# Four of the 23 word conversions moved beside the second expert, the rest spread evenly

## The chip, the cores and the metric

The program runs on one core of one Trainium2 chip. The metric is device microseconds of one execution. Three executions of the kernel before gave 713.09, 840.9 and 712.39 us; the median is 713.09 us. All times inside the kernel come from one further, profiled execution.

## The reference, cut to what matters

Three stages follow one another. A gated linear attention makes x, 3072 tokens of 384 numbers. A mixture of eight experts sends each token to the one with the largest gate logit. A gated perceptron takes the result of that:

```python
# mixture of experts, for the tokens of expert e
h = np.maximum(x[mask] @ w1[e], 0.0)            # 384 -> 1024
out[mask] = gate_w[mask, None] * eom[mask, e, None] * (h @ w2[e])   # 1024 -> 384
# perceptron
a = x @ w1; b = x @ w2                          # 384 -> 1024 each
out = ((a * b) @ w3) @ w_out                    # 1024 -> 1024 -> 384
```

The perceptron's four weights reach the kernel as 64-bit floats. Each has to be rebuilt as a 32-bit float from its high and its low word before it can be used; this is the word conversion that the change moves.

## The kernel before, in words

**Arithmetic.** Every product after the attention is made with three matmuls of a high and a low part (`mm3`, L168 to L171). So each weight tile is split first: `feed` (L150) copies a 128x768 tile on ScalarE (L159) and subtracts on VectorE (L160). Activations are split in the same way (`x_split` L845 and L846, `h_split` L854 and L855).

**Order.** The order of every engine's instructions is the order in which the Python program emits them; nothing is reordered later. Each engine works through its own queue in that order, and the first instruction that waits holds all behind it. The SyncE queue (SP) issues the loads in the same way, and GpSimd (POOL) issues the gathers and the stores of converted words.

**The loop over experts (L1077).** Expert `e` has eight steps "up" (`e_up`, nine matmuls each, into one of three PSUM tiles `u`) and eight steps "down" (`e_down`, nine matmuls each). The number of columns falls from 464 to 360 with the expert (`CAPS`). In the down steps f = 1, 3 and 5 the tokens of the next expert are transposed on TensorE and split; the up steps of the next expert need all three. Expert 0 has its up steps elsewhere. After expert 6, `w_prime` (L1041) multiplies w3 and w_out into `wpr`, 64 blocks of three matmuls. Then comes expert 7, and then the perceptron (L1172), which is TensorE alone but for small work beside it.

**Side work.** Between steps, `next(conv)` emits the next piece of a generator. During experts 0 and 1 that is `late_routing` (gates, one-hot tiles `sohl` on VectorE at L715, and a sorting product on TensorE at L722, which is emitted in down step 5 of expert 1). From expert 2 on it is `convert_all`: 23 conversions in turn, each in four pieces:

- piece 1: ScalarE takes the absolute value of the high words (L132, "Abs");
- piece 2: VectorE clamps, shifts and joins them (L134, L135, L136, "the join");
- piece 3: nothing;
- piece 4: ScalarE scales the low words (L139), SP issues the load for the conversion after next (L958), GpSimd adds (L141) and issues the store of the tile to `wm_d` in DRAM (L962).

The raw words come into two buffers (`mr`), the results lie in two (`cva`), the scaled low words in one (`cvc`). The converted tiles are read back from `wm_d` by L120, from expert 5 on, as the weights of `w_prime` and of the perceptron. Before the change, a piece is emitted at each of the 16 steps of experts 2 to 4, at 12 of the 16 steps of experts 5 and 6, at every second block of the first three rows of `w_prime`, and at three blocks in eight of the next four. So experts 2, 3 and 4 hold four conversions each, experts 5 and 6 three, and the rest falls to `w_prime`.

**Rooms.** `wpr` has the pool `wprp` (L673) to itself, 12 KB of each partition, and is not written before `w_prime`. After expert 1 the routing's pools are closed (L1118) and the conversion's buffers take their place.

Of the kernel before, what the change touches and what calls it, by code (L numbers as in the profile page):

```python
# [7 lines left out]
F32 = mybir.dt.float32  # L8
F32R = mybir.dt.float32r
BF16 = mybir.dt.bfloat16  # L10
I32 = mybir.dt.int32
U32 = mybir.dt.uint32
ACTF = mybir.ActivationFunctionType
ALU = mybir.AluOpType
# [9 lines left out]
E = 8  # L24
F = 1024
KF = F // 128
# [5 lines left out]
TINY = 2.0 ** -15  # L32
NPC = 768
# [2 lines left out]
DP = 64  # L36
NP = 3
N_WO, N_W3, N_M, N_RING = 4, 11, 8, 8
N_D = N_WO + N_W3 + N_M

GMX = 6
# [15 lines left out]
def attention_then_moe_kernel(ctx, tc, pk0, pka, pkb, wbd_d, wexp, wmlp, cst_d, out):  # L57
    nc = tc.nc
    V, A, G, T, SP = nc.vector, nc.scalar, nc.gpsimd, nc.tensor, nc.sync
# [18 lines left out]
    jxB = const.tile([128, NJ], BF16, name="jxB")  # L78
    wm_d = dram.tile([N_D, 128, NPC], F32, name="wm_d")
    x_d = dram.tile([NTOK, DM], F32, name="x_d")  # L80
# [12 lines left out]
    def runits(a, b):  # L93
        return [("r", i, dkeys[i:min(i + 2, b)]) for i in range(a, b, 2)]

    def sunits(e):
        return [("s", 4 * e + u, [("e", e, 2 * u), ("e", e, 2 * u + 1)]) for u in range(4)]

    units = [u for e in range(E - 1) for u in sunits(e)] + runits(0, N_WO + N_W3)
    units += sunits(E - 1) + runits(N_WO + N_W3, N_D)  # L100
    Y_FIRST, Y_END = 6, len(units) - (N_M + 1) // 2
    assert Y_END % 4 == 0
    stream = [(u, c, key) for u, un in enumerate(units) for c, key in enumerate(un[2])]
    wmlp_w = wmlp.bitcast(I32)
# [3 lines left out]
    def load_ahead():  # L108
        while loaded[0] < min(freed[0] + (4 if Y_FIRST <= loaded[0] < Y_END + 2 else pools["keep"]), pools["upto"]):
# [14 lines left out]
            raws[loaded[0]] = raw  # L124
            loaded[0] += 1

    def words(raw, read):
        w = raw.rearrange("p (n t) -> p n t", t=2)
        lw, hw = w[:, :, 0], w[:, :, 1]
        a, c = [pools["cv"].tile([128, NPC], I32, tag=t, name="cv" + t, bufs=n) for t, n in (("a", 2), ("c", 1))]  # L130
        af = a.bitcast(F32)
        A.activation(out=af, in_=hw.bitcast(F32), func=ACTF.Abs)  # L132
        yield
        V.tensor_scalar(out=af, in0=af, scalar1=TINY, scalar2=None, op0=ALU.max)  # L134
        V.tensor_scalar(out=a, in0=a, scalar1=3, scalar2=0x3FFFFFF8, op0=ALU.logical_shift_left, op1=ALU.bitwise_and)  # L135
        V.scalar_tensor_tensor(out=a, in0=hw, scalar=-(1 << 30), in1=a, op0=ALU.bitwise_and, op1=ALU.bitwise_or)  # L136
        yield
        yield
        A.activation(out=c, in_=lw.bitcast(U32), func=ACTF.Copy, scale=2.0 ** -29)  # L139
        read()  # L140
        G.tensor_tensor(out=a, in0=a, in1=c, op=ALU.add)  # L141
        return a.bitcast(F32)
# [412 lines left out]
    for j in range(NJ):  # L555
# [30 lines left out]
        if j == 5:  # L586
            A.activation(out=row, in_=cst[:, C_E4:C_E4 + E], func=ACTF.Copy, scale=1024.0)
            V.scalar_tensor_tensor(out=revc, in0=cst[:, C_E4:C_E4 + E], scalar=-1024.0 * E, in1=rev, op0=ALU.mult,
                                   op1=ALU.add)
# [27 lines left out]
    def k_up(q, fs=range(2), low_last=False):  # L617
# [4 lines left out]
        for part in ((0, 1), (2,)) if low_last else ((0, 1, 2),):  # L622
            for f, k, sl in blocks:
                for i in part:
# [31 lines left out]
                    op=ALU.mult)  # L656
# [3 lines left out]
    for q in range(1, 4):  # L660
# [3 lines left out]
                    op=ALU.is_equal)  # L664
# [8 lines left out]
    wpr_p = ctx.enter_context(tc.tile_pool(name="wprp", bufs=1, reuse_waits="tile"))  # L673
# [9 lines left out]
    def rtile(shape, name, dt=F32):  # L683
        return rt_p.tile(shape, dt, name=name)
# [121 lines left out]
    def places(os_, big):  # L806
        V.tensor_scalar(out=zs, in0=zs, scalar1=1.0, scalar2=None, op0=ALU.add)
        yield
        V.tensor_tensor(out=pos, in0=pos, in1=key, op=ALU.add)
        V.reciprocal(out=zs, in_=zs)  # L810
        yield
        V.tensor_tensor(out=zs, in0=zs, in1=se, op=ALU.mult)
        yield
        sp = [rtile([128, NJ], f"sp{i}", BF16) for i in range(3)]
        V.tensor_copy(out=sp[0], in_=zs)
        yield
        V.tensor_tensor(out=zs, in0=zs, in1=sp[0], op=ALU.subtract)
        yield
        V.tensor_copy(out=sp[1], in_=zs)
        yield  # L820
        V.tensor_tensor(out=zs, in0=zs, in1=sp[1], op=ALU.subtract)
        yield
        V.tensor_copy(out=sp[2], in_=zs)
        yield
        yield from onehots(pos, iotaB[:, 0:NJ], sp, "s", os_, big)
# [55 lines left out]
    for f in range(KF):  # L881
        w = pieces["e", 0, f // 2]
# [21 lines left out]
    def late_routing(big):  # L904
        os_ = []
        yield from gates()
        yield from places(os_, big)
        yield
        yield
        ps_o = ps_u.tile([128, CMX], F32, tag="u", name="u")[:, 0:5 * NJ].rearrange("p (n h) -> p n h", n=5)  # L910
        sorted_mm(ps_o.rearrange("p n h -> p (n h)"), *os_)
        so = rtile([128, 5, NJ], "so")
        A.activation(out=so, in_=ps_o, func=ACTF.Copy)
        V.scalar_tensor_tensor(out=idx_o, in0=so[:, 0, :], scalar=128.0, in1=so[:, 1, :], op0=ALU.mult, op1=ALU.add)
        G.tensor_tensor(out=s2, in0=so[:, 2, :], in1=so[:, 3, :], op=ALU.add)
        G.tensor_tensor(out=s2, in0=s2, in1=so[:, 4, :], op=ALU.add)
        G.tensor_tensor(out=s2, in0=s2, in1=s2, op=ALU.mult)
# [34 lines left out]

    mraw = {}

    def m_load(i):
        if i < N_D:
            mraw[i] = pools["mr"].tile([128, 2 * NPC], I32, tag="mr", name="mraw")
            SP.dma_start(out=mraw[i], in_=wmlp_w[i])  # L958
# [82 lines left out]
    def w_prime():  # L1041
        wpr = wpr_p.tile([128, KF, DM], F32, tag="wpr", name="wpr")
        for f in range(KF):
            ps = ps_u.tile([128, CMX], F32, tag="u", name="u")[:, 0:DM]
            for g in range(KF):
                blk = f * KF + g
                hl, o = pieces["3", blk // 6], slice(blk % 6 * 128, blk % 6 * 128 + 128)
                so = slice(g % 2 * DM, (g % 2 + 1) * DM)
                wo = pieces["o", g // 2]
                mm3(ps, hl[:, 0, o], hl[:, 1, o], wo[:, 0, so], wo[:, 1, so], g == 0, g == KF - 1)  # L1050
                if blk % 6 == 5:
                    pieces.pop(("3", blk // 6))
                    if blk // 6 < N_W3 - 4:
                        feed(1)
                if f == KF - 1 and g % 2:
                    pieces.pop(("o", g // 2))
                    feed(1)
                if g % 2 if f < 3 else f < KF - 1 and g in (1, 4, 7):
                    next(conv, None)
            A.activation(out=wpr[:, f], in_=ps, func=ACTF.Copy)  # L1060
        pieces.pop(("3", N_W3 - 1))
        return wpr


    pl_p = lr.enter_context(tc.tile_pool(name="pl", bufs=1, reuse_waits="tile"))
    conv = late_routing(pl_p.tile)
    cv2 = ExitStack()

    def convert_all():
        m_load(0)  # L1070
        m_load(1)
        for _ in range(3):
            yield
        for i in range(N_D):
            yield from m_convert(i)

    for e in range(E):  # L1077
        if e == 1:
            interleave(windows())
        for f in range(KF if e else 0):  # L1080
            e_up(e, f, pieces["e", e, f // 2])
            if f % 2:
                pieces.pop(("e", e, f // 2))
            if (f % 2 if e < E - 1 else 3 <= f < 7):
                feed(1)
            if e < 5 or e < E - 1 and f % 2 == 0:
                next(conv, None)
        if e == E - 1:
            col = off_of(e)
            for d in range(KD):  # L1090
                feed((2, 2, 0)[d])
                for f in range(KF):
                    e_down(e, f, pieces["e", e, 4 + f // 2], [d])
                e_store(e, col, [d])
                y_split(0, [d])
            for f in range(4):
                pieces.pop(("e", e, 4 + f))
            break
        if e == 0:
            feed(1)  # L1100
        for f in range(KF):
            e_down(e, f, pieces["e", e, 4 + f // 2])
            if f % 2:
                pieces.pop(("e", e, 4 + f // 2))
                feed(1)
            if e == 0 and f in (0, 2) or 2 <= e < 6 and f == 4:
                feed(1)
            for _ in range(1 if e else 1 + f % 2):
                next(conv, None)
            if f in (1, 3, 5):  # L1110
                x_split(e + 1, f // 2, xg[e + 1])
                if f == 5 and e + 2 < E and e != 1:
                    x_gather(e + 2)
        e_store(e, off_of(e))
        if e == 1:
            for _ in conv:
                pass
            lr.close()  # L1118
            all_overflows()
            x_gather(e + 2)  # L1120
            pools["cv"] = cv2.enter_context(tc.tile_pool(name="cvb", bufs=1, reuse_waits="tile"))
            pools["mr"] = cv2.enter_context(tc.tile_pool(name="mr", bufs=2, reuse_waits="tile"))
            conv = convert_all()
        if e == E - 2:
            wpr = w_prime()
# [136 lines left out]
```

## Time and profile before

| what | value |
|---|---|
| median of three executions | 713.09 us |
| the profiled execution | 716.86 us, of which the span from first to last instruction is 714.8 us |
| TensorE busy | 678.5 us, 95% of the span |
| VectorE, ScalarE, GpSimd busy | 401.4, 339.0, 205.7 us |
| mean granted clock of TensorE | 0.978 |
| expert 1, its up and down steps | 174.1 to 206.5 us |
| experts 2 to 6 | 206.5 to 346.7 us |
| `w_prime` | 346.7 to 381.8 us |
| expert 7 | 381.8 to 407.8 us |
| perceptron | 407.8 us to the end |

A start is given in us from the first instruction. A granted clock of 1.00 is 2.4 GHz and 0.50 is 1.2 GHz. Matmuls overlap in their pipeline, so that the distance between the starts of two matmuls is what one costs, not its listed duration.

### The profile page before, as it was taken

How to read it: one execution, taken by the hardware profiler on the slowest of the kernel's cores; microseconds unless marked ns; L12 is line 12 of the kernel's file. 1: busy time of each engine (PE TensorE's matmuls, PEld its weight loads, DVE VectorE, ACT ScalarE, POOL GpSimd, SP SyncE). 2: the span in 40 equal slices, each digit the busy share in tenths (PEclk: the TensorE clock that was granted, in tenths of full speed). 3: DMA queues.
4: the chain of work that ended last, by engine and by line, in shares of the span. 5: the costliest groups of instructions: out<-in, count | busy, mean ns of one | idle time of the engine just before them, and what ended most of it. 6: DMA issues, size and time to landing. Idle time of an engine off the chain costs nothing.

```text
span 714.8 us, 14636 instructions
## 1 busy us (share of the span) xinstructions
PE 678.5 (95%) x5904; PEld 614.7 (86%) x5904; DVE 401.4 (56%) x746; ACT 339.0 (47%) x676; POOL 205.7 (29%) x231
## 2 busy tenths in 40 slices
PE   6999997979999999999998999999999999999993
PEld 3878886868999998999998988989889889889893
DVE  7989997755948799877648564032132231340320
ACT  3888885434446667666655554123222222231220
POOL 2978775240223463451443000101101002001001
PEclk8999998989999999999999999999999999999997
DMA  9899886345257889878786200100000000001000
GB/s 287 228 270 264 263 251 210 126 137 221 89 163 277 312 297 329 309 268 296 270 287 221 88 1 1 44 1 12 33 1 23 22 1 34 12 0 45 1 11 33
DMA packets 28326, 102.53 MB, mean 143 GB/s; under 512 B 4736, under 2 KB 5120, under 8 KB 28256
## 3 DMA queue, kind: packets, MB, share of 16 engines
q1 hardware_dynamic: 21360, 77.26, 33.3%
q0 software_dynamic: 6752, 24.12, 9.7%
q8 instruction: 47, 0.77, 0.5%
q14 instruction: 23, 0.19, 0.1%
q10 hardware_dynamic: 144, 0.20, 0.1%
HBM read 83.07 MB, written 18.48 MB: 142 GB/s over the span
## 4 chain that ended last, share of the span: by engine, by line
PE 57%; DMA 6%; issue 2%; ACT 2%; DVE 2%; POOL 1%; POOLq 0%; ACTq 0%
PE pab L169 9%; PE pab L170 9%; PE pab L171 9%; PE o L170 4%; PE o L171 4%; PE o L169 4%; DMA mraw<-in_wmlp_dram 3%; PE u L169 3%; PE u L171 3%; PE u L170 3%; PE d L170 3%; PE d L169 3%; PE d L171 3%; DMA wm_d<-cva 2%; ACT w L159 1%
## 5 line engine op out<-in xcount | busy, mean ns | idle before, releaser
L1155 DVE TENSOR_TENSOR p_s<-pab,a_s 128x512 f32<-128x512 f32 x48 | 33.2, 692 | 162.7 <-PE pab L171 160.4
L170 PE MATMUL pab<-y,w 128*128 128x512 f32 x288 | 112.0, 389 | 0.0
L169 PE MATMUL pab<-y,w 128*128 128x512 f32 x288 | 112.0, 389 | 0.0
L171 PE MATMUL pab<-y,w 128*128 128x512 f32 x288 | 112.0, 389 | 0.0
L1169 POOL DMA_INDIRECT out_dram<-o_s,idx_o x24 | 23.2, 969 | 297.2 <-ACT o_s L1168 292.7
L160 DVE TENSOR_TENSOR w<-raw,w 128x768 fp32r<-128x768 f32 x87 | 97.8, 1131 | 18.1 <-ACT w L159 16.1
L1157 ACT ACTIVATE ab<-p_s 128x512 fp32r<-128x512 f32 x48 | 30.3, 632 | 102.4 <-DVE p_s L1155 102.4
L159 ACT ACTIVATE w<-raw 128x768 fp32r<-128x768 f32 x87 | 71.7, 838 | 9.9 <-PE d L171 9.5
L169 PE MATMUL d<-h,w 128*128 128x464 f32 (+7 forms) x192 | 69.6, 363 | 4.0 <-ACT w L159 4.0
L141 POOL TENSOR_TENSOR cva<-cva,cvc 128x768 int32<-128x768 int32 x23 | 47.2, 2053 | 87.3 <-ACT cvc L139 51.3
L171 PE MATMUL d<-h,w 128*128 128x464 f32 (+7 forms) x192 | 67.9, 354 | 0.0
L170 PE MATMUL d<-h,w 128*128 128x464 f32 (+7 forms) x192 | 67.8, 353 | 0.0
L169 PE MATMUL o<-wpp,ab 128*128 128x384 f32 x192 | 64.2, 334 | 0.0
L171 PE MATMUL o<-wpp,ab 128*128 128x384 f32 x192 | 64.2, 334 | 0.0
L170 PE MATMUL o<-wpp,ab 128*128 128x384 f32 x192 | 64.2, 334 | 0.0
L171 PEld LDWEIGHTS pab<-y,w 128*128 128x128 f32 x288 | 54.1, 188 | 11.3
L169 PEld LDWEIGHTS pab<-y,w 128*128 128x128 f32 x288 | 54.1, 188 | 11.0
L170 PEld LDWEIGHTS pab<-y,w 128*128 128x128 f32 x288 | 54.1, 188 | 11.0
L169 PE MATMUL u<-xt,w 128*128 128x448 f32 (+6 forms) x168 | 59.0, 351 | 4.2 <-DVE h L855 2.4
L171 PE MATMUL u<-xt,w 128*128 128x448 f32 (+6 forms) x168 | 58.5, 348 | 0.4 <-DVE w L160 0.4
L170 PE MATMUL u<-xt,w 128*128 128x448 f32 (+6 forms) x168 | 58.5, 348 | 0.3 <-DVE xt L846 0.3
L1158 DVE TENSOR_TENSOR ab<-p_s,ab 128x512 fp32r<-128x512 f32 x48 | 33.2, 692 | 33.5 <-ACT ab L1157 33.5
(239 smaller groups left out, 1480.6 us busy)
## 6 DMA issues: line engine op xcount, KB each, us to landing
raw<-in_wexp_dram SPq DMA_DIRECT2D x32, 768.0 KB, 5.6
mraw<-in_wmlp_dram SPq DMA_DIRECT2D x23, 768.0 KB, 6.4
pb<-in_pkb_dram SPq DMA_DIRECT2D x24, 384.0 KB, 5.1
wm_d<-cva POOLq DMA_DIRECT2D x23, 384.0 KB
raw<-wm_d SPq DMA_DIRECT2D x23, 384.0 KB, 5.3
pa<-in_pka_dram SPq DMA_DIRECT2D x42, 192.0 KB, 4.5
x_d<-xs POOLq DMA_DIRECT2D x23, 192.0 KB
pa<-in_pka_dram SPq DMA_DIRECT2D x42, 97.5 KB, 5.5
```

The source lines that it names most:

```text
L141: G.tensor_tensor(out=a, in0=a, in1=c, op=ALU.add)
L159: A.activation(out=hl[:, 0], in_=src, func=ACTF.Copy)
L160: low = lambda: eng.tensor_tensor(out=hl[:, 1], in0=src, in1=hl[:, 0], op=ALU.subtract)
L169: T.matmul(out=ps, lhsT=sh, rhs=mh, start=start, stop=False)
L170: T.matmul(out=ps, lhsT=sh, rhs=ml, start=False, stop=False)
L171: T.matmul(out=ps, lhsT=sl, rhs=mh, start=False, stop=stop)
L1155: V.tensor_tensor(out=p_s, in0=pss[1], in1=a_s, op=ALU.mult)
L1157: A.activation(out=t[:, 0], in_=p_s, func=ACTF.Copy)
L1158: V.tensor_tensor(out=t[:, 1], in0=p_s, in1=t[:, 0], op=ALU.subtract)
L1169: G.indirect_dma_start(out=out[:, :], out_offset=bass.IndirectOffsetOnAxis(ap=idx_o[:, n:n + 1], axis=0), in_=o, in_offset=None)
```

## The change

A second generator, `first_words`, makes the first four conversions in expert 1. Its raw words, its scaled low words and one of its two results lie in the pool of `wpr`; the other result is in the routing's pool. There is one buffer for raw words, so the load of the next conversion waits until the join and the scaling of this one have read it. Its first piece is emitted in down step 6 of expert 0 and the other sixteen in the sixteen steps of expert 1, each behind the piece of `conv` and, in down steps, ahead of `x_split`. Both ScalarE operations are in the first piece of a conversion, the join, the addition and the next load in the second, nothing in the third, and the store in the fourth.

`convert_all` begins at conversion 4. Its pieces come at 12 steps of each of the experts 2 to 6, which is three conversions per expert, and in `w_prime` at three blocks in eight of the first six rows and at one block of the seventh.

```diff
+N_FIRST = 4
...
+    def high_words(a, hw):
+        af = a.bitcast(F32)
+        V.tensor_scalar(out=af, in0=af, scalar1=TINY, scalar2=None, op0=ALU.max)
+        V.tensor_scalar(out=a, in0=a, scalar1=3, scalar2=0x3FFFFFF8, op0=ALU.logical_shift_left, op1=ALU.bitwise_and)
+        V.scalar_tensor_tensor(out=a, in0=hw, scalar=-(1 << 30), in1=a, op0=ALU.bitwise_and, op1=ALU.bitwise_or)
...
+    def first_words():
+        room = wpr_p.tile([128, 4, NPC], I32, tag="wpr", name="room")
+        raw, c = room[:, 0:2].rearrange("p a n -> p (a n)"), room[:, 2]
+        w = raw.rearrange("p (n t) -> p n t", t=2)
+        lw, hw = w[:, :, 0], w[:, :, 1]
+        av = [pl_p.tile([128, NPC], I32, name="fwa"), room[:, 3]]
+        SP.dma_start(out=raw, in_=wmlp_w[0])
+        yield
+        for i in range(N_FIRST):
+            a = av[i % 2]
+            A.activation(out=a.bitcast(F32), in_=hw.bitcast(F32), func=ACTF.Abs)
+            A.activation(out=c, in_=lw.bitcast(U32), func=ACTF.Copy, scale=2.0 ** -29)
+            yield
+            high_words(a, hw)
+            G.tensor_tensor(out=a, in0=a, in1=c, op=ALU.add)
+            if i + 1 < N_FIRST:
+                SP.dma_start(out=raw, in_=wmlp_w[i + 1])
+            yield
+            yield
+            G.dma_start(out=wm_d[i], in_=a.bitcast(F32))
+            yield
...
-                if g % 2 if f < 3 else f < KF - 1 and g in (1, 4, 7):
+                if f < KF - 2 and g in (1, 4, 7) or f == KF - 2 and g == 1:
                     next(conv, None)
...
-        for i in range(N_D):
+        for i in range(N_FIRST, N_D):
             yield from m_convert(i)
...
-            if e < 5 or e < E - 1 and f % 2 == 0:
+            if e < 2 or e < E - 1 and f % 2 == 0:
                 next(conv, None)
+            if e == 1:
+                next(firsts, None)
...
             for _ in range(1 if e else 1 + f % 2):
                 next(conv, None)
+            if e == 1 or (e, f) == (0, KF - 2):
+                next(firsts, None)
...
         if e == 1:
-            for _ in conv:
+            for _ in (*conv, *firsts):
                 pass
```

## Rows read from the trace of the kernel before

**Rows 1.** The page's first part: busy us, share of the span, instructions of each engine.

```profile
PE 678.5 (95%) x5904; PEld 614.7 (86%) x5904; DVE 401.4 (56%) x746; ACT 339.0 (47%) x676; POOL 205.7 (29%) x231
```

**Rows 2.** Stretches (experts 1, 4, 5, 6): length, busy PE, PEld, DVE, ACT, POOL, clock, DMA.

```profile
174.10:206.50 32.40, 32.11 (x182) 29.28 (x181) 21.63 (x51) 14.82 (x26) 5.31 (x7) 1.00 0.31 100
264.10:293.90 29.80, 28.02 (x158) 26.89 (x157) 28.95 (x36) 20.72 (x33) 16.42 (x14) 1.00 0.92 336
293.90:320.30 26.40, 26.40 (x155) 26.29 (x154) 21.78 (x29) 16.34 (x27) 10.92 (x10) 1.00 0.79 267
320.30:346.70 26.40, 25.85 (x155) 25.44 (x154) 18.92 (x28) 17.12 (x28) 7.18 (x7) 1.00 0.84 299
```

**Rows 3.** Waits of TensorE from 206 to 408 us: total us, times, longest.

```profile
PE u L169 <- DVE h L855: 2.4, 4, 0.9
```

**Rows 4.** TensorE in order of time, 378 to 387 us: start, us, instruction, idle before.

```profile
379.98 0.34 PE L171 MATMUL u<-w,w 128*128 128x384 f32 x1
381.86 0.43 PE L169 MATMUL u<-xt,w 128*128 128x360 f32 x1 [1.54 <-ACT w L159]
...
382.85 0.67 PE L171 MATMUL u<-xt,w 128*128 128x360 f32 x1 [0.40 <-DVE w L160]
383.32 0.50 PE L169 MATMUL u<-xt,w 128*128 128x360 f32 x1
```

**Rows 5.** ScalarE in order of time, 371 to 382 us.

```profile
379.78 0.92 ACT L139 ACTIVATE cvc<-mraw 128x768 int32<-128x768 uint32 x1 [2.56 <-POOL cva L141]
...
380.98 1.57 ACT L159 ACTIVATE w<-raw 128x768 fp32r<-128x768 f32 x2
```

**Rows 6.** Tiles cva and mraw: duration ns min/median/max, first and last start; landing us.

```profile
L132 ACT ACTIVATE cva<-mraw x23: 889/903/924, 216.4 to 375.9; 128x768 f32<-128x768 f32 x23
L134 DVE TENSOR_SCALAR cva<-cva x23: 544/552/2207, 218.3 to 378.0; 128x768 f32<-128x768 f32 x23
L135 DVE TENSOR_SCALAR cva<-cva x23: 559/561/725, 218.8 to 380.2; 128x768 int32<-128x768 int32 x23
L136 DVE SCALAR_TENSOR_TENSOR cva<-mraw,cva x23: 957/959/961, 219.4 to 380.8; 128x768 int32<-128x768 int32 x23
L141 POOL TENSOR_TENSOR cva<-cva,cvc x23: 1823/1865/2583, 220.5 to 381.9; 128x768 int32<-128x768 int32 x23
...
DMA to landing us min/median/max: 4.1/6.4/9.0
```

**Rows 7.** Tile raw in expert 1 (174 to 206 us): landing of the weight loads.

```profile
DMA to landing us min/median/max: 4.3/4.3/4.3
```

**Rows 8.** VectorE in order of time, expert 1.

```profile
180.31 0.17 DVE L823 CAST sp<-zs 128x24 bf16<-128x24 f32 x1
...
194.00 0.95 DVE L160 TENSOR_TENSOR w<-raw,w 128x768 fp32r<-128x768 f32 x1
...
195.52 0.59 DVE L846 TENSOR_TENSOR xt<-x,xt 128x424 fp32r<-128x424 f32 x1
196.03 0.73 DVE L715 TENSOR_SCALAR sohl<-iotaB,slo 128x128 bf16<-128x128 bf16 x4
```

**Rows 9.** TensorE in order of time, 199 to 208 us.

```profile
200.68 1.43 PE L722 MATMUL u<-srhs,sohl 128*128 128x120 bf16 x24
...
206.51 0.43 PE L169 MATMUL u<-xt,w 128*128 128x424 f32 x1 [0.30 <-PEq L1011]
```

**Rows 10.** VectorE, then GpSimd, in order of time, 271 to 274.5 us.

```profile
271.86 2.40 DVE L160 TENSOR_TENSOR w<-raw,w 128x768 fp32r<-128x768 f32 x1
...
271.61 1.84 POOL L141 TENSOR_TENSOR cva<-cva,cvc 128x768 int32<-128x768 int32 x1 [2.62 <-ACT cvc L139]
```

**Rows 11.** TensorE at 154.68 us, and two stretches with the granted clock (column before last two).

```profile
154.68 0.75 PE L169 MATMUL d<-h,w 128*128 128x464 f32 x1 [4.04 <-ACT w L159]
...
155.00:161.00 6.00, 6.00 (x16) 4.77 (x16) 4.80 (x10) 2.65 (x5) 0.00 (x0) 0.51 0.39 131
383.00:386.00 3.00, 3.00 (x10) 3.00 (x11) 3.00 (x2) 1.86 (x4) 2.04 (x2) 0.50 0.06 25
```

More of the change, by code (lines that the diff above doesn't have):

```diff
@@ L130, in words @@
         a, c = [pools["cv"].tile([128, NPC], I32, tag=t, name="cv" + t, bufs=n) for t, n in (("a", 2), ("c", 1))]
-        af = a.bitcast(F32)
-        A.activation(out=af, in_=hw.bitcast(F32), func=ACTF.Abs)
+        A.activation(out=a.bitcast(F32), in_=hw.bitcast(F32), func=ACTF.Abs)
         yield
-        V.tensor_scalar(out=af, in0=af, scalar1=TINY, scalar2=None, op0=ALU.max)
-        V.tensor_scalar(out=a, in0=a, scalar1=3, scalar2=0x3FFFFFF8, op0=ALU.logical_shift_left, op1=ALU.bitwise_and)
-        V.scalar_tensor_tensor(out=a, in0=hw, scalar=-(1 << 30), in1=a, op0=ALU.bitwise_and, op1=ALU.bitwise_or)
+        high_words(a, hw)
         yield
@@ L953, in attention_then_moe_kernel @@
     mraw = {}
+    def first_words():
[8 more added lines that the diff above has]
+            a = av[i % 2]
+            A.activation(out=a.bitcast(F32), in_=hw.bitcast(F32), func=ACTF.Abs)
+            A.activation(out=c, in_=lw.bitcast(U32), func=ACTF.Copy, scale=2.0 ** -29)
+            yield
+            high_words(a, hw)
+            G.tensor_tensor(out=a, in0=a, in1=c, op=ALU.add)
[5 more added lines that the diff above has]
+            yield
     def m_load(i):
@@ L1066, in attention_then_moe_kernel @@
     conv = late_routing(pl_p.tile)
+    firsts = first_words()
     cv2 = ExitStack()
     def convert_all():
-        m_load(0)
-        m_load(1)
+        m_load(N_FIRST)
+        m_load(N_FIRST + 1)
         for _ in range(3):
             yield
-        for i in range(N_D):
+        for i in range(N_FIRST, N_D):
             yield from m_convert(i)
```

## The prediction, made before the change was run

> **What bounds the kernel now.** I read the engine totals first. TensorE is busy for 95% of the span [rows 1], so only a microsecond in which it waits can be won, and every new wait is lost. I then read the stretches of the experts, to see where it waits. In expert 1 it is busy for 32.11 of 32.40 us, and the engines beside it have room: VectorE 21.63, ScalarE 14.82, GpSimd 5.31, DMA at a share of 0.31. Expert 4, with four conversions, keeps TensorE for 28.02 of 29.80 us, with VectorE at 28.95 and DMA at 0.92. Expert 5, with three, loses nothing, and expert 6, also with three, loses 0.55 [rows 2]. The waits name who is late: `h_split` on VectorE, four times, 2.4 us in all [rows 3]. The order of TensorE shows the last place, the start of expert 7, where it waits 1.54 us for a ScalarE weight copy, 0.40 for its VectorE half, and then runs at a start every 0.30 us [rows 4] with a granted clock of 0.50, which is the 1.2 GHz level [rows 11]. Behind that is ScalarE, which stood 2.56 us at the last conversion's L139, held by GpSimd's addition, with the four weight copies queued behind it [rows 5].
>
> **What the change can win.** The idle time is 2.4 us [rows 3], 0.3 for the rest of expert 4's 1.78 [rows 2], and 1.54 + 0.40 at expert 7 [rows 4], 4.6 us together. A wait costs about 0.17 more than its idle time: 381.86 - 379.98 = 1.88 us between starts, where 0.17 is a matmul and 1.54 the idle part [rows 4]. Seven waits make that 1.2. The half clock covers about ten matmuls, with 0.30 - 0.165 us lost on each, say 1.6 with its first slow one. The ceiling is 7.4 us. By place: experts 3 and 4 about 3.0, expert 6 0.7, expert 7 3.7.
>
> - *Experts 2 to 4* go from four conversions to three. That is the load of expert 5, which lost nothing [rows 2]. I take the whole 3.0.
> - *Expert 6* keeps three; I take half, 0.3.
> - *Expert 7.* The last piece moves from the second-last place of the seventh row of `w_prime` to its first block, and a conversion comes every 1.33 rows from the start, where before it came every row for three rows. So ScalarE should be through with L139 before the first of the copies for expert 7, in row eight. I take 3.3 of 3.7.
>
> The sum of the gains is 6.6 us, with ends at 0 and 7.4. Fewer loads under experts 2 to 6 are in this sum already; the dropped pieces cost TensorE nothing where it did not wait.
>
> **What it costs in expert 1.** Four conversions bring eight ScalarE operations of 0.90 us, twelve VectorE operations, 0.55 + 0.56 + 0.96 = 2.07 per join, four GpSimd additions of 1.87 [rows 6], four loads on SP and four stores on GpSimd. By totals they fit: VectorE 21.6 + 8.3 of 32.4, ScalarE 14.8 + 7.2 [rows 2, 6]. But there is one raw buffer, so the conversions are a chain: load, Abs, join, load. Bare, a round is 4.3 [rows 7] + 0.90 + 2.07 + some 0.3 of hand-overs = 7.6 us; the four steps it is given are a quarter of the 32.4 us of expert 1 [rows 2] less some 3 of sorting and transposes, 7.4. There is no slack for standing in a queue, and each piece stands behind what was emitted before it. I walked the queues by hand, with the durations of before:
>
> - *Conversion 0.* Its load is emitted early enough to be there. The join is queued behind L823, which was done at 180.5 [rows 8]; it ends at 182.6. Load 1 then goes out, and lands at 186.9.
> - *Conversion 1.* Both ScalarE operations run to 188.7. Behind them stand a relu and a weight copy (0.8, [rows 5]), then on VectorE the weight's low half (0.95) and four one-hot tiles (0.73) [rows 8]. The join ends at 193.7, load 2 lands at 198.0.
> - *Conversion 2.* ScalarE to 199.8, weight copy to 200.6, low half to 201.6, one-hots to 202.3, join to 204.4. Behind that join, in VectorE's queue, stand the split of the first transpose (0.59) and the last four one-hots (0.73) [rows 8], ready at 205.7. The sorting product needs them; it began at 200.68 [rows 9], so TensorE stands **5.0 us**. Load 3 lands at 208.7.
> - *Conversion 3.* Its Abs stands in ScalarE's queue ahead of a weight copy and the third `x_split`. ScalarE to 210.4, copies and split to 212.0, low half and join to 214.4, split of the third transpose to 215.0. Expert 2 needs it, and began at 206.51 [rows 9]: **8.5 us** late in all.
>
> A round is thus some 10.6 us, not 7.4. SP is not the brake: its weight loads behind `first_words`' loads wait for later VectorE work anyway. GpSimd's gather for expert 3 comes behind the last addition, some 10 us later than before, but has all up steps of expert 2 as cover; without that cover it would cost the same 10 us. The stores have a round or more before their buffer is wanted again.
>
> *The shared port.* A weight half that meets an addition took 2.40 us in place of 0.95, and ended 0.81 after the addition [rows 8, 10]. With three additions in the chain that is 0 to 3 × 1.45 = 4.3 us; I take 2.0, as not every addition will meet one. The Trainium skill (SBUF — State Buffer, on contention at the shared port) has it that whichever of the two starts first holds the other fully; by that an addition can as well be the one that waits, the port term would be 0 where it always is, and the sum 3.5 us in place of 5.5.
>
> *The clock.* After 4.04 us of idle TensorE ran at 0.51 for the six us looked at, after two waits together of 1.94 us at 0.50 for three [rows 11, 4]; the 0.91 us wait of expert 4 left it at 1.00 [rows 2, 3]. The 5 us stand at the sorting product is followed by steps that end before the third split in any case, so that its slow matmuls are hidden. The second stand, about 3 us, is not: 1.6 (three us at half clock) to 3.3 (six and a half), or 0 if the clock stays; I take 1.6. The Trainium skill (TensorE: Matmul & The Clock Gate, on HAM oscillation) says that an array that keeps waiting for operands pays the cold start at every wait; by that the first stand pays too and the sum would be 1.6 higher.
>
> The loss: 8.5 + 2.0 + 1.6 = 12.1 us. The net: 12.1 - 6.6 = **+5.5 us**. The sum is made against the profiled execution, 716.86 us, whose span is 714.8; its own time lies 3.8 above the median of the runs. The difference is taken to the median: 713.1 + 5.5 = **718.6 us**. Ends: loss 8 without port and clock, up to 8.5 + 4.3 + 3.3 = 16.1 with both; gains 7.4 or 3.0. That is +1 to +13 with the landing of 4.3 kept.
>
> **Rivals.**
>
> - *The cover holds.* If VectorE comes to the joins without the queueing of the walk, a round is its bare 7.6 us, the loss is three times 0.2 us and a hand-over, about 1, and the gains stand: 713.1 + 1 - 7.4 = 706.7. For it: the totals fit. Against it: the order is fixed, and the pieces stand between the weights and the one-hots.
> - *Slow landing, slower than before.* The same load took 6.4 us in the median beside other conversions, 9.0 at most [rows 6]. At 6.4, three loads add 6.3 us to the chain; 18.4 - 3.0 is 15.4 more, 728.5. It decides from about 6 us of landing in expert 1. For it: the new loads meet weight loads and stores. Against it: the DMA share there is 0.31, and its loads landed in 4.3 [rows 2, 7].
> - *The end is not relieved*: the change does not do what "fewer at the end" says, as ScalarE is still behind from waiting for `wm_d` stores. Then 3.3 is missing, 722. For it: `w_prime` still holds five conversions with two result buffers. Against it: the last L139 is emitted two blocks of time earlier, and it stood by 2.56 us only [rows 5].
>
> **How the numbers follow.** Forecast 0.52, end not relieved 0.18, cover holds 0.15, slow landing 0.13, others 0.02. The range goes from 708, into the case that the cover holds, to 727, past the unrelieved end and into the slow landing. Two per cent, about what a measurement of this kernel can tell from no change, is 14.3 us. Faster by that is beyond the ceiling: 0.02. Slower by that is most of the slow landing: 0.09. Within: 0.89.
>
> **What would show it.** Right: TensorE waits at L722 for a one-hot tile and at expert 2's first matmul for VectorE's split, about 10 us together, with ScalarE idle before L132 of conversions 1 to 3 until a load; no waits on `h_split` in experts 3 and 4; at most some tenths before expert 7. Wrong: expert 2 starts by 208 us, or rounds of conversions 0 to 3 take 7 to 8 us; or the stalls of experts 3 and 4 stay although their conversions are fewer.

## The result, and the profile after

| | before | changed |
|---|---|---|
| median, runs on the same chip | 712.75 us | 720.39 us |
| ratio of the two | | 1.011, 95% interval 1.008 to 1.014 |
| profiled execution, its span | 716.86, 714.8 us | 718.12, 716.0 us |
| the same on a second chip, median | 705.63 us | 714.26 us, ratio 1.012 (1.008 to 1.016) |

The kernel became about 1% slower. The medians are over all executions; the ratios, here and below, leave out the few that ran in a slower state, such as the one of 840.9 us. The table below gives the length of each stage in profiled executions, from the start of its first matmul to that of the next. The second execution of each kernel, on another chip, is beside the first in brackets.

| stage | before | changed | difference of the first two |
|---|---|---|---|
| expert 1 | 32.32 (32.33) | 43.46 (43.46) | +11.14 |
| expert 2 | 29.11 (29.15) | 30.68 (30.64) | +1.57 |
| expert 3 | 28.57 (28.30) | 27.91 (27.94) | -0.66 |
| expert 4 | 29.79 (29.75) | 27.22 (27.26) | -2.57 |
| expert 5 | 26.37 (27.18) | 26.37 (26.36) | 0 |
| expert 6 | 26.40 (26.08) | 26.08 (26.08) | -0.32 |
| `w_prime` | 35.11 (34.74) | 33.29 (33.29) | -1.82 |
| expert 7 | 25.96 (26.00) | 23.67 (23.68) | -2.29 |
| experts 1 to 7 | 233.63 (233.53) | 238.68 (238.71) | +5.05 |

Expert 1 lost 11.1 us and expert 2 1.6; everything behind them won 7.7. Below, "the stretch" is the sum in the last line, which repeated within 0.1 us where a kernel was profiled twice. In the changed kernel the lines of code stand further down: L159, L160, L715, L722, L846, L855 and L1011 of before are L163, L164, L719, L726, L850, L859 and L1037. `first_words` has its Abs at L969, addition at L973, loads at L975, stores at L978; its join is L130 to L132.

The engine totals of the changed kernel, to be held against [rows 1], say almost nothing, since the work is the same:

```profile
PE 674.7 (94%) x5904; PEld 613.2 (86%) x5904; DVE 403.7 (56%) x746; ACT 339.4 (47%) x676; POOL 204.5 (29%) x231
```

The stretches say more. Of the changed kernel, experts 1, 2, 4, 5 and 6, with the columns of [rows 2]:

```profile
169.85:213.31 43.46, 35.27 (x182) 30.89 (x180) 34.27 (x62) 20.45 (x34) 15.38 (x14) 0.92 0.47 157
213.31:243.99 30.68, 30.68 (x156) 29.69 (x157) 20.15 (x26) 16.73 (x27) 11.99 (x11) 0.94 0.75 255
271.90:299.12 27.22, 27.22 (x157) 27.10 (x157) 23.34 (x30) 18.02 (x30) 11.17 (x10) 1.00 0.82 293
299.12:325.49 26.37, 26.37 (x154) 26.26 (x154) 21.38 (x29) 16.27 (x27) 10.57 (x10) 1.00 0.80 260
325.49:351.57 26.08, 25.84 (x154) 25.43 (x154) 18.91 (x28) 17.04 (x28) 7.17 (x7) 1.00 0.84 305
```

TensorE is idle for 8.2 us of expert 1, and for none of experts 2, 4 and 5. Where it waits, from 165 to 216 us and then from 213 to 410 us (line waited at, whose tile, total, times, longest):

```profile
PE u L173 <- DVEq L1037: 4.2, 1, 4.2
PE u L726 <- DVE sohl L719: 3.8, 1, 3.8
...
PE u L173 <- DVE h L859: 0.2, 1, 0.2
```

So the waits on `h_split` of [rows 3] are gone but for 0.2 us, and two new ones stand in expert 1. TensorE in order of time shows both, what the clock does behind them, and the start of expert 7, where [rows 4] had the slow stretch:

```profile
196.79 1.84 PE L726 MATMUL u<-srhs,sohl 128*128 128x120 bf16 x20
202.46 0.77 PE L726 MATMUL u<-srhs,sohl 128*128 128x120 bf16 x4 [3.83 <-DVE sohl L719]
...
208.69 0.37 PE L175 MATMUL d<-h,w 128*128 128x448 f32 x1
213.31 0.43 PE L173 MATMUL u<-xt,w 128*128 128x424 f32 x1 [4.25 <-DVEq L1037]
...
216.31 0.56 PE L173 MATMUL u<-xt,w 128*128 128x424 f32 x1
216.67 0.55 PE L174 MATMUL u<-xt,w 128*128 128x424 f32 x1
217.02 0.39 PE L175 MATMUL u<-xt,w 128*128 128x424 f32 x1
...
384.68 0.33 PE L175 MATMUL u<-w,w 128*128 128x384 f32 x1
384.86 0.32 PE L173 MATMUL u<-xt,w 128*128 128x360 f32 x1
385.02 0.32 PE L174 MATMUL u<-xt,w 128*128 128x360 f32 x1
```

The sorting product began nearly in time, 26.9 us into expert 1 where it was 26.5 before. It ran 20 of its 24 matmuls and stood for the last four one-hot tiles. Expert 2 began 4.6 us behind the start of the last down matmul. Until 217 us its matmuls then start every 0.355 us, where 0.195 is the rate after that. Expert 7 follows `w_prime` without a gap and at full clock.

The other engines tell why. The next four views show, each in order of time, SP's loads, ScalarE's Abs that waits for one, VectorE, and GpSimd:

```profile
178.43 0.34 SPq L975 DMA_DIRECT2D room<-in_wmlp_dram  x1
190.05 0.34 SPq L975 DMA_DIRECT2D room<-in_wmlp_dram  x1
200.47 0.34 SPq L975 DMA_DIRECT2D room<-in_wmlp_dram  x1
```

```profile
194.28 0.91 ACT L969 ACTIVATE fwa<-room 128x768 f32<-128x768 f32 x1 [6.66 <-DMA room<-in_wmlp_dram]
204.79 0.90 ACT L969 ACTIVATE room<-room 128x768 f32<-128x768 f32 x1 [6.54 <-DMA room<-in_wmlp_dram]
```

```profile
190.43 2.07 DVE L719 TENSOR_SCALAR sohl<-iotaB,slo 128x128 bf16<-128x128 bf16 x4
...
199.45 0.96 DVE L132 SCALAR_TENSOR_TENSOR fwa<-room,fwa 128x768 int32<-128x768 int32 x1
200.32 0.59 DVE L850 TENSOR_TENSOR xt<-x,xt 128x424 fp32r<-128x424 f32 x1
200.83 2.06 DVE L719 TENSOR_SCALAR sohl<-iotaB,slo 128x128 bf16<-128x128 bf16 x4
...
209.45 0.96 DVE L132 SCALAR_TENSOR_TENSOR room<-room 128x768 int32<-128x768 int32 x1
210.33 0.59 DVE L850 TENSOR_TENSOR xt<-x,xt 128x424 fp32r<-128x424 f32 x1
210.84 2.27 DVE L164 TENSOR_TENSOR w<-raw,w 128x768 fp32r<-128x768 f32 x1
```

```profile
190.11 1.84 POOL L973 TENSOR_TENSOR room<-room 128x768 int32<-128x768 int32 x1 [3.66 <-issue]
200.56 1.79 POOL L973 TENSOR_TENSOR fwa<-fwa,room 128x768 int32<-128x768 int32 x1 [7.71 <-DVE fwa L132]
210.49 1.80 POOL L973 TENSOR_TENSOR room<-room 128x768 int32<-128x768 int32 x1 [0.99 <-DVE room L132]
```

Joins end at 178.35, 189.98, 200.41 and 210.41 us, and each load goes out within 0.1 us of a join's end. ScalarE stands in the second and the third load wait, and everything queued on it stands too. The third join ends at 200.41, when the sorting product has run out of tiles (at 198.6); the one-hots behind it are held by the addition (2.06 us in place of the 0.73 of [rows 8]). The fourth join ends at 210.41, the third split of the tokens at 210.92. TensorE still does not start. It waits for L1037, which is `with tc.If(n_ov > 0)` in `all_overflows`, the branch ahead of expert 2. Instructions of that line in the changed kernel, with the time of first and last start at the end:

```profile
L1037 PEldq EVENT_SEMAPHORE  x1: 51/51/51, 209.1 to 209.1; - x1
...
L1037 DVEq EVENT_SEMAPHORE  x1: 21/21/21, 213.1 to 213.1; - x1
```

TensorE is at the branch at 209.1. VectorE gets there at 213.1, when it has done all that was emitted ahead of the branch; the last of it is the weight half at 210.84, which the addition holds, so that it ends at 213.11. Before, TensorE came there later than VectorE:

```profile
L1011 DVEq EVENT_SEMAPHORE  x1: 21/21/21, 205.1 to 205.1; - x1
...
L1011 PEldq EVENT_SEMAPHORE  x1: 51/51/51, 206.3 to 206.3; - x1
```

### The profile page after: what moved, and what is told of

Read it like the earlier page. It is cut to its first block, busy times and chain, and to the rows that moved or that the text cites. A ratio compares the mean times of both kernels' runs of the same rounds, so it can differ in the third digit from the quotient of the medians.

```text
span 716.0 us, 14629 instructions
## 1 busy us (share of the span) xinstructions
PE 674.7 (94%) x5904; PEld 613.2 (86%) x5904; DVE 403.7 (56%) x746; ACT 339.4 (47%) x676; POOL 204.5 (29%) x231
## 4 chain that ended last, share of the span: by engine, by line
PE 67%; issue 1%; ACT 0%; DMA 0%; DVE 0%; POOLq 0%; ACTq 0%
PE pab L173 9%; PE pab L175 9%; PE pab L174 9%; PE u L173 5%; PE u L174 5%; PE u L175 5%; PE o L175 4%; PE o L173 4%; PE o L174 4%; PE d L174 4%; PE d L175 4%; PE d L173 4%; PE x L836 1%; DMA out_dram<-o_s,idx_o 0%; ACT yT L945 0%
## 5 line engine op out<-in xcount | busy, mean ns | idle before, releaser
L164 DVE TENSOR_TENSOR w<-raw,w 128x768 fp32r<-128x768 f32 x87 | 95.6, 1104 | 27.6 <-ACT w L163 25.0
L163 ACT ACTIVATE w<-raw 128x768 fp32r<-128x768 f32 x87 | 71.8, 840 | 15.3 <-PE d L175 9.5
L145 POOL TENSOR_TENSOR cva<-cva,cvc 128x768 int32<-128x768 int32 x19 | 36.8, 1938 | 88.1 <-ACT cvc L143 83.9
```

What stands on the lines that cost most here:

```text
L163: A.activation(out=hl[:, 0], in_=src, func=ACTF.Copy)
L164: low = lambda: eng.tensor_tensor(out=hl[:, 1], in0=src, in1=hl[:, 0], op=ALU.subtract)
```

## The experiments

The experiments ran on three chips, each compared with the kernel before on its own: the gains alone, the cost alone, the loads and "spread" on one, the additions on a third, all others on the one that the first table calls the second. Stage lengths are those of the profiled executions, as above. "Base" is the kernel before: 32.32 us for expert 1, 233.63 or 233.53 for the stretch.

**The gains alone.** The four conversions are replaced by four plain copies of raw words.

```diff
         for i in range(N_FIRST):
-            a = av[i % 2]
...
-            G.dma_start(out=wm_d[i], in_=a.bitcast(F32))
+            SP.dma_start(out=wm_d[i], in_=wmlp_w[i][:, 0:NPC].bitcast(F32))
             yield
```

> The four conversions beside expert 1 are left out (a copy in DRAM fills their place in wm_d, so the first four weight tiles are wrong); everything from expert 2 on is as in the changed kernel. Theory (the loss lies in expert 1, and the relief of experts 3, 4 and 7 is worth 7.5 us): expert 2 starts as in the kernel before, no waits of TensorE on h_split in experts 3 and 4 and none before expert 7, 705.5 us or a ratio of 0.990 (0.986 to 0.993). Rival (the later relief came only because expert 2 started late, with VectorE and the transfers given 9 us to catch up): the waits in experts 3, 4 and 7 are back for at least 4 us, ratio 0.995 or more.

Measured: 704.58 us, ratio 0.990 (0.986 to 0.994); the stretch 225.96, 7.7 below base. Expert 1 as a window, to be held against the first line of [rows 2]:

```profile
169.35:201.67 32.32, 32.02 (x182) 29.23 (x180) 21.59 (x50) 14.73 (x26) 5.31 (x7) 1.00 0.41 138
```

Three conversions in each of experts 2 to 6, and four fewer in all, are worth 7.7 us, 3.2 of it in experts 3 and 4 and 4.1 at the end. Expert 2 starts as before here, so its late start is not what the gain needs. All of the loss hangs on the conversions in expert 1.

**The cost alone.** `first_words` stays, and conversions 4 to 22 come at the old places.

```diff
-                if f < KF - 2 and g in (1, 4, 7) or f == KF - 2 and g == 1:
+                if g % 2 if f < 3 else f < KF - 1 and g in (1, 4, 7):
...
-            if e < 2 or e < E - 1 and f % 2 == 0:
+            if e < 5 or e < E - 1 and f % 2 == 0:
```

> Expert 1 as in the changed kernel, but the conversions 4 to 22 come at the old steps: four per expert in experts 2 to 4, and they are through early in w_prime. Theory (pace): expert 1 loses the same 11 us and some 1.5 of half clock; the waits of experts 3 and 4, some 3 us, are back; no wait before expert 7. Ratio 1.012 to 1.016. Rival (four conversions fewer in the whole queue relieve experts 3 and 4 whatever the pace): no such waits, ratio 1.005 to 1.009.

Measured: 722.18 us, ratio 1.012 (1.009 to 1.015); the stretch 240.60, 7.0 above base. TensorE from 220 to 410 us:

```profile
PE u L173 <- DVE h L859: 1.8, 3, 0.9
```

Expert 4 is back at 29.27 us, expert 3 stays at 27.92, `w_prime` and expert 7 stay relieved. So the pace gives expert 4's 2.0 us, less than the 3 expected. The 4.1 at the end come with four fewer conversions to do, whatever the pace. Expert 3 is another matter: its four conversions stand at the same steps as before, so neither the pace nor a smaller number relieved it here. Expert 2 starts some 9 us late in this kernel, with more cover for VectorE and the transfers; whether that did it was not shown.

**The loads.** Loads 1 to 3 are left out, and the first raw words are used four times.

```diff
             G.tensor_tensor(out=a, in0=a, in1=c, op=ALU.add)
-            if i + 1 < N_FIRST:
-                SP.dma_start(out=raw, in_=wmlp_w[i + 1])
             yield
```

> As the changed kernel, but the loads of the raw words 1 to 3 beside expert 1 are left out: all four conversions there read the first raw words, so three weight tiles are wrong. Theory A (the chain through the single raw buffer is the whole loss): a round of conversions falls to the 7.4 us of its four steps, ScalarE no longer waits before its Abs, expert 1 loses 1 us or less, ratio 0.990 to 0.993. Theory B (the joins stand ahead of the last one-hot tiles and the splits in VectorE's queue, which is almost full): the third join still ends behind 198 us on the clock of the kernel before, TensorE still waits 3 to 4 us at the sorting product, expert 1 loses 4 to 5 us, ratio 0.995 to 0.999.

Measured: 714.20 us, ratio 1.003 (1.000 to 1.005); the stretch 232.53, expert 1 38.81. The loads are worth 4.65 us of expert 1 and, the wait at the branch being shorter, the 1.5 of half clock in expert 2 (29.11): 6.2 together. The other 6.5 of expert 1 stays, with 2.8 us at the sorting product and 1.8 at the branch. Neither expectation fits. ScalarE shows a second chain that I had not written down, on the one buffer of scaled low words:

```profile
194.34 0.90 ACT L970 ACTIVATE room<-room 128x768 int32<-128x768 uint32 x1 [3.56 <-POOL room L973]
...
203.11 0.91 ACT L970 ACTIVATE room<-room 128x768 int32<-128x768 uint32 x1 [4.76 <-POOL fwa L973]
```

**The additions.** The same without GpSimd's additions, to part that chain and the port from VectorE's queue.

```diff
             high_words(a, hw)
-            G.tensor_tensor(out=a, in0=a, in1=c, op=ALU.add)
-            if i + 1 < N_FIRST:
-                SP.dma_start(out=raw, in_=wmlp_w[i + 1])
             yield
```

> Conversions 0 to 3 without loads 1 to 3 and without GpSimd's addition, so that what is stored is the joined high words only; the rest as changed. Without the loads expert 1 still took 38.81 us in place of 32.32, and ScalarE stood 3.56 and 4.76 us before its scaling of the low words, for the addition of the conversion before. Theory A (additions: the one buffer of scaled low words makes a second chain, and the additions hold VectorE's operations at the port): expert 1 takes 32.3 to 34 us, with at most 1 us of waiting at the sorting product and before expert 2; from expert 1 to the perceptron 226 to 228 us, the ratio 0.988 to 0.994. Rival B (VectorE's queue: the joins stand ahead of the one-hots whatever comes after them): expert 1 takes 36 us or more, the sorting product still waits 2 us or more; 230 us or more, the ratio 0.995 to 1.002.

Measured: 702.10 us, ratio 0.996 (0.993 to 0.999); expert 1 33.44, the stretch 227.10. No wait is left at the sorting product, and 1.39 at the branch. VectorE does all four joins in the same queue places here, so with ScalarE's eight operations their room costs 1.1 us at most. A holds by the stages, though the wait at the branch is above its 1 us; the ratio lies above what A gave, which belongs to the open point below. Loads 4.65, additions 5.4, and 1.1 for the rest make the 11.1 of expert 1, taken out in this order; what the additions cost with the loads in place was not run. Nor was how the 5.4 divide between the scaling's wait and the port.

**The branch.** `all_overflows()` is left out, and with it the handling of tokens beyond an expert's columns; there are none in these inputs.

```diff
             lr.close()
-            all_overflows()
             x_gather(e + 2)
```

> As the changed kernel, but the branch behind expert 1, the handling of experts with more tokens than their room (not taken with these inputs), is left out. Theory (expert 2 was held by the meeting of the engines at the branch: VectorE gets there only when the last weight half of expert 1, held behind GpSimd's addition, is done, and posts its event then): expert 2 starts when the third split is done, 2 us earlier, loss in expert 1 some 9 us in place of 11, ratio 1.006 to 1.009. Rival (expert 2 was held by the third split, as the prediction had it, and the event only came last by chance): expert 2 starts as late as before, ratio 1.010 to 1.012.

Measured: 707.62 us, ratio 1.003 (1.001 to 1.005); the stretch 233.58, which is 5.1 below the changed kernel: 3.56 in expert 1 (39.90), 1.5 in expert 2 (29.20, no half clock). VectorE in this kernel, where expert 2 began at 203.96:

```profile
203.92 0.96 DVE L132 SCALAR_TENSOR_TENSOR room<-room 128x768 int32<-128x768 int32 x1
204.80 0.59 DVE L850 TENSOR_TENSOR xt<-x,xt 128x424 fp32r<-128x424 f32 x1
205.30 2.31 DVE L164 TENSOR_TENSOR w<-raw,w 128x768 fp32r<-128x768 f32 x1
```

Expert 2 started 0.8 us *before* the third split began and 3.6 before the weight half was done. It needs neither to start. So the branch, and not the split that the prediction named, held it. TensorE did not wait ahead of expert 2 at all; it came there 7.6 us late, by the stand at the sorting product and the slow matmuls behind that, which nothing covers here.

**Spread.** Conversions six steps apart over experts 0 and 1, with three steps for each landing.

```diff
-        yield
+        for _ in range(3):
+            yield
...
             G.dma_start(out=wm_d[i], in_=a.bitcast(F32))
-            yield
+            for _ in range(3):
+                yield
...
-            if e == 1 or (e, f) == (0, KF - 2):
+            if e <= 1:
                 next(firsts, None)
```

> As the changed kernel, but the first four conversions are spread over the 24 steps of experts 0 and 1, six steps apart, with the same single raw buffer; the load of the first is emitted in the first down step of expert 0. Theory (rounds need some 10.5 us and get 7.4): six steps are 11 us, so the chain fits, the sorting product and expert 2 are late by 2 us or less, the gains stay, ratio 0.990 to 0.994. Rival (expert 0's down steps have no room: VectorE is busy for 8.2 of 12 us there and the gathers and loads share the transfers): expert 1 starts 3 us or more late, ratio 0.998 to 1.005.

Measured: 705.63 us, ratio 0.990 (0.987 to 0.994); the stretch 229.20, 4.4 below base. No wait is left at the sorting product. Expert 1 takes 35.56: 1.1 us on a split in its up steps, behind a weight half that an addition held (2.35 us), and the branch. Run once more on the second chip:

> Four conversions six steps apart over experts 0 and 1, once more on the same chip: 229 us from expert 1 to the perceptron; ratio 0.988 to 0.994 if the waits of the kernel before are there, near 1.000 if they are not.

Measured: 706.21 us, ratio 1.001 (0.998 to 1.003), with a stretch of 229.23. The stretch repeated; the ratio did not.

**Five steps apart**, three to land; as "spread", with `range(2)` behind the store.

```diff
-            yield
+            for _ in range(2):
+                yield
```

> Five steps apart, first conversion three steps after its load, both from expert 0 on; the last join stands in down step 3 of expert 1. Five steps are 9.2 us against rounds of 10 to 11.6 in the changed kernel. Theory (what counts is the lag of the chain against its steps, which grows by 1 to 2 us per round): expert 1 loses 1 to 3 us at the sorting product or the split, and nothing at the branch, ratio 0.989 to 0.993. Rival (VectorE alone counts, and its work is the same): as the run with six steps, ratio 0.990 with the 2 us at the branch.

Measured: 705.79 us, ratio 1.000 (0.998 to 1.002); the stretch 230.85. Nothing waits at the sorting product, but 3.2 us at the branch, and half clock behind it (expert 2 30.62). VectorE's last pieces ahead of the branch are late again, one of them a weight half of 2.37 us that the last addition held. The rival is nearer as to the place; the ratio is above both.

**Six apart, begun earlier**, with one step to land; the rest as in "spread".

```diff
-        yield
+        for _ in range(1):
+            yield
...
+    next(firsts)
     for e in range(E):
```

> As the run with the four conversions six steps apart over experts 0 and 1, but the first load is emitted ahead of the loop and the first conversion begins in the first down step of expert 0, so that the last join stands in down step 5 of expert 1, three steps earlier than there. Theory (there the 2.2 us before expert 2 were the last join ahead of the branch): that wait falls to 1 us or less, ratio 0.987 to 0.990 against the kernel before. Rival (expert 0 is where it hurts: the first conversion on ScalarE stands ahead of weight copies that TensorE waits for at the start of the down steps): expert 1 starts 1.5 us or more later than in that run, ratio 0.991 to 0.995.

Measured: 708.17 us, ratio 1.003 (1.001 to 1.006); the stretch 233.13. Where TensorE waits from 165 to 220 us, and what held ScalarE:

```profile
PE u L173 <- DVE h L859: 4.3, 1, 4.3
PE u L173 <- DVEq L1039: 0.4, 1, 0.4
```

```profile
167.05 0.90 ACT L970 ACTIVATE room<-room 128x768 f32<-128x768 f32 x1 [4.10 <-DMA room<-in_wmlp_dram]
```

The wait at the branch is gone, as expected. In its place a load issued at 159.72 took 7.3 us to land beside expert 0's loads; the Abs that waited for it held a weight copy and the splits of expert 1's up steps. VectorE then had the join ahead of those splits, and an operation on 8 numbers that the addition held to 1.77 us. One step is too little there: a miss for the total.

**Three conversions** in `first_words`, six apart, four under expert 2; the rest as in "spread".

```diff
-N_FIRST = 4
+N_FIRST = 3
...
-            if e < 2 or e < E - 1 and f % 2 == 0:
+            if e < 3 or e < E - 1 and f % 2 == 0:
```

> Three conversions beside experts 0 and 1, six steps apart, and four in expert 2, which lost nothing with four in the kernel before. Theory (what is left of the loss is the last join ahead of the branch and VectorE's full queue in expert 1): no wait at the branch, 1 us or less in expert 1, 226 to 228 us from expert 1 to the perceptron, 2 us less than with four; ratio 0.984 to 0.991 if the waits of the kernel before are there. Rival (expert 2 with four conversions brings back waits in expert 3): as the run with four.

Measured: 703.53 us, ratio 0.998 (0.995 to 1.000); the stretch 230.51. Expert 1 is down to 33.82 and the branch costs 0.3, as it should. But expert 2 takes 32.22, with a new wait and a slow clock behind it:

```profile
198.65 0.36 PE L175 MATMUL u<-xt,w 128*128 128x424 f32 x1
200.31 0.46 PE L173 MATMUL u<-xt,w 128*128 128x424 f32 x1 [1.30 <-issue]
```

What TensorE waited for is not in the trace. This is the lowest median of the variants on the second chip, 0.25% below the kernel before, with an interval that touches 1; "spread" won 1% on one chip and nothing on the other. So no version was shown to beat the kernel before.

**Both kernels again**, on the second chip.

> The kernel before once more, for its trace beside the following ones on one chip. From the first matmul of expert 1 to the perceptron it should take 233.6 us again, with its waits in experts 3, 4 and 7; if it takes 230 or less on this chip, the gain of the other kernels is smaller here, since the waits came from transfers that land sooner. Ratio 1.000.

> The changed kernel once more, on the same chip as the kernel before: 238.7 us from expert 1 to the perceptron, 11 us lost in expert 1; ratio 1.007 to 1.011 if the waits of the kernel before are there, 1.012 or more if they are not.

Measured: 706.48 us for the kernel before, ratio to itself 1.000 (0.998 to 1.003), and 714.26 for the changed one, 1.012 (1.008 to 1.016). The stage lengths stand in brackets in the first section; the waits of the kernel before were there on this chip too.

**What stays open.** The stretch gives the changed kernel +5.1 us and the end of the perceptron another 0.4; the medians give 7.6 and 8.6. Most of the variants, too, stand 1 to 3 us higher in their ratios than in their stretch ("spread" on the second chip by 4.8, on the first 1.9 lower; the additions by 3.8). The gains alone, without the work of `first_words`, stand only 0.5 higher. As the stretch and the end repeat where they were profiled twice, the missing time should lie ahead of expert 1, but no trace shows it there. Expert 1 begins anywhere from 164 to 174 us in the profiled executions, at 174.19 in the kernel before, where a wait of 4.04 us and a half clock precede it [rows 11], and at 167.94 in its second. The two profiled executions of before were 3.8 and 4.0 us above their medians, so they don't stand for its usual start. Whether the first load of `first_words`, which goes out at 163.26 us in the changed kernel, 6.6 us ahead of expert 1, has a part in this was not shown.

## Why the prediction was right, and where it was not

*The bound.* Right for the stretch: the totals hardly moved, and what came or went there shows as waits of TensorE and slow matmuls behind them.

*Experts 3 and 4, 6, 7.* Predicted 3.0, 0.3 and 3.3; measured 3.2, 0.3, and 4.1 with the end of `w_prime`. The sum, 6.6, was 1.1 too small; 7.7 is a little above even the ceiling of 7.4. With the gains alone it was also 7.7. Two of the reasons were partly others. With the old pace expert 7's relief came as well, so that four fewer conversions do it, and not the place of the last pieces; and expert 3 was relieved with four conversions in it, too. Expert 6's 0.3 agrees by luck: on the second chip expert 6 won nothing, and expert 5 won 0.8.

*The chain in expert 1.* Right to some tenths. Between the two profiled executions expert 1 begins 4.3 us earlier. The walk's join ends, less 4.3, are 178.3, 189.4, 200.1 and 210.1; measured 178.35, 189.98, 200.41 and 210.41. Rounds are 11.6, 10.4 and 10.0 us, against 10.6. Loads landed within 4.2 to 4.8 us (load out to Abs), against 4.3, so that slow landing and the holding cover both fell. The sorting product stood 3.8 us, against 5.0, and two errors are in that. The walk let the whole product stand from its start, but 20 of its matmuls, 1.84 us, ran first; and the tiles it stood for came some 1.1 us later than in the walk (202.46 against 201.4), as the addition held them.

*What holds expert 2: the step that failed.* The prediction put it as "split of the third transpose to 215.0. Expert 2 needs it". The split came at 210.92, which is 215.2 on the old scale, but without the branch TensorE started before it. The kernel before could have told: in expert 4, which began at 264.19, TensorE waits for the low half of the third split only at its eighth matmul:

```profile
265.94 0.45 PE L170 MATMUL u<-xt,w 128*128 128x396 f32 x1 [0.32 <-DVE xt L846]
```

The holder was the branch, where TensorE waits for the event of VectorE and so for *all* that VectorE had queued ahead of it. The same pair shows in four kernels: VectorE's event at 213.1, 210.8 (no loads), 200.8 (spread) and 202.5 us (five), and expert 2 at 213.31, 211.01, 200.99 and 202.71. I had seen the line in [rows 9], as a wait of 0.30, and gave it no part. That the number survived is luck: the branch asks for the end of the same queue, 2.2 us later than the split. In the run without the branch expert 2 was 7.6 us late, by TensorE's own delay, and not by the split.

*The port.* Predicted 2.0 of 0 to 4.3. Four of VectorE's operations in expert 1 were held by an addition, and lost 1.4, 1.34, 1.33 and 1.3 us (1.60 against 0.17, 2.07 and 2.06 against 0.73, 2.27 against 0.95). The first, behind conversion 0's addition, is none of the weight halves that the prediction reckoned with:

```profile
178.80 1.60 DVE L704 TENSOR_SCALAR shi<-pos 128x24 int32<-128x24 f32 x1
```

What the first two cost the chain was not shown. The third delayed the one-hots that the sorting product stood for. The last lay at the branch and counted in full, together with the 0.95 of the half itself; 8.5 + 2.0 stood for the 11.1 measured. The Trainium skill (SBUF — State Buffer, on contention at the shared port) lets either side be held; in expert 1 the additions always started first and kept their 1.79 to 1.84 us, and the term was not 0. The other side shows in "spread", where a weight half that had started first kept its time and the addition took 2.42 us:

```profile
199.83 0.95 DVE L164 TENSOR_TENSOR w<-raw,w 128x768 fp32r<-128x768 f32 x1
...
200.06 2.42 POOL L974 TENSOR_TENSOR room<-room 128x768 int32<-128x768 int32 x1 [3.10 <-DVE room L132]
```

*The clock.* Predicted 1.6 behind the second stand; measured nine matmuls at 0.355 in place of 0.195 us, 1.45. Slow matmuls followed the first stand too, as the Trainium skill (TensorE: Matmul & The Clock Gate, on HAM oscillation) has it. Two stretches of the changed kernel, one behind each stand, the columns as above:

```profile
202.46:205.50 3.04, 3.04 (x13) 2.69 (x14) 1.81 (x5) 0.71 (x1) 0.56 (x1) 0.50 1.04 362
...
213.31:217.02 3.71, 3.71 (x11) 3.51 (x12) 0.00 (x0) 0.46 (x1) 1.42 (x2) 0.55 0.91 318
```

But those slow matmuls ended at 207 us and the last down step at 209, and the branch opened at 213. They were hidden, as the prediction said, though by another cover than it named; without the branch they were not.

*The second chain.* The prediction counted only the raw buffer. The scaled low words have one buffer too, and ScalarE stands for the addition of the conversion before; without the loads this becomes the limit.

*The end not relieved.* Fell: 3.3 was won and more.

*The sum.* Predicted 12.1 lost and 6.6 won, +5.5. Measured 12.7 lost (11.1 + 1.6) and 7.7 won, +5.05 in the stretch. The forecast case came true in size and in most of its signs: the two waits of expert 1 were 8.1 us together, where about 10 was named, and the second was at the branch. The median's further 2 to 3 us are the open point.

## What to carry to other kernels

Where a chain of load, ScalarE, VectorE and load goes through queues with other work in them, walk the queues with the durations of the trace; the sum of busy times gives no hint of a round of 10 us where the parts make 7.6. At a branch one engine may have to wait for the whole queue of another, as TensorE here for VectorE's. Look which work is emitted just ahead of it, and keep optional work away, since even an operation that nobody needs yet is then on the path. And before moving side work to an engine's "room", look for every single buffer in it, as each makes a chain of its own.

## What the runs showed that I had not expected

- An operation of VectorE that an addition of GpSimd holds goes on when the addition ends, whatever its own size: four one-hot tiles, 0.73 us together, took 2.07, an operation on 128x24 numbers 1.60. The 13 weight halves of the kernel before that started during an addition took 1.12 to 2.58 us, and each ended 0.81 to 0.82 us after it.
- Not all of VectorE's work is held. The low halves of `h_split` and `x_split`, which read PSUM, started during an addition 10 times in the kernel before, and none was longer for it (0.54 to 0.58 us). No join's L132 met an addition in any trace here, so its steady 0.96 us says nothing of the port.
- Without the branch the changed kernel is level with the one before in its stretch, 233.58 against 233.53 us: here an `If` whose body is never run costs 5.1 us, as TensorE comes to it 4 us ahead of VectorE.
